# A spectral filter and a SwiGLU block in float32: two plain stripes at the start, and another share-out of the splits

## The chip, the cores and the metric

The kernel runs on one core of one Trainium2 chip. The metric is the device time of one execution in microseconds. Five engines work on their own queues: TensorE (PE, with its weight loads shown as PEld), VectorE (DVE), ScalarE (ACT), GpSimd (POOL) and SyncE (SP), which here only issues DMAs.

## The reference, cut to what matters

```python
# x: (8, 3008, 256) float32; filt_r, filt_i: (1505, 256)
X = np.fft.rfft(x, axis=1)
y = np.fft.irfft(X * (filt_r + 1j * filt_i)[None], n=3008, axis=1).astype(np.float32)
t = y.reshape(24064, 256)
g = t @ w_gate                      # w_gate, w_val: (256, 1536), w_out: (1536, 256)
silu = g * (1.0 / (1.0 + np.exp(-g)))
out = (silu * (t @ w_val) @ w_out).astype(np.float32)
```

Each batch of 3008 tokens is filtered along the sequence, then every token goes through a gated feed-forward block. The three weight matrices arrive as 64-bit floats.

## The kernel before

**The block.** The 24064 tokens are cut into 47 stripes of T = 512 tokens, the 1536 hidden columns into ND = 12 slices of 128. One stripe with one slice is a unit; there are 564. A unit does three things: `gate` (the first product, t with the slice of w_gate), `value` (t with the slice of w_val, then the Silu and the product h of both) and `project` (h times the slice of w_out, summed in PSUM over the 12 units of a stripe). The main loop goes over n and works on unit n, on the split of unit n-1 and on the projection of unit n-2.

**Triples.** The fast matmul form takes float32r, which holds fewer bits than float32. So each operand is kept as three tiles: a high part hi, a low part lo, and a combination both. Of a product of two triples, the matmuls with hi and lo go into one PSUM bank and those with the combination into another, and ScalarE (a scaling by 1/LAM) and VectorE (`axpy`, line 235) put the two together. A unit therefore has 18 matmuls of 128x128 by 128x512: ws (line 888) and wx (892) in `gate` and `value`, six each, and six in `project` (928, 930, 932). For the activations the split is: ACT scales h to hh (hi), POOL subtracts to get hl (lo, line 229), DVE's axpy makes hs (both). `split` issues the first two a unit later, `split_rest` the third two units later. The token stripes are split the same way by `split_y` into yh, yl, ys.

**PSUM.** Four banks (pool wps) serve the unit's products and the transforms, four (pool ops) the projections. Which of the four a product gets is left to the allocator; it is no fixed turn.

**Weights.** Preparation turns 64-bit weights into float32 and splits them into triples: 36 halves (12 slices by three matrices), each of 128x256, in a chain of small steps (lines 275 to 302 on DVE, 280 to 295 on ACT, 306 on POOL, then three split steps). Steps are spread over ticks: 44 ticks in the head, then three per unit. The first N_EARLY = 9 halves are loaded into the still empty y_t, the later ones into rt just before their use. Eight slices have a slot on chip (gv_t, wo_t); six of the twelve are written to DRAM (gv_all, wo_all) and streamed back for every stripe into two slots, by SP, a few units ahead.

**The early part.** Because the weights come slowly, the first FIRST = 5 stripes (batch 0 nearly whole) are visited in NG = 3 phases of DG = 4 slices: units 0 to 59. Between the phases the partial sums of a stripe go to DRAM (o_dram), come back (`load_before`) and are added on POOL (`join`).

**The transform.** Batch 0 is transformed first, alone, as matrix products (`stage1_first`, `turn`, `stage2a`, `stage2b`, `stage3`); stage3 has four quarters k, each writing every fourth group of eight tokens of y_t, so all four are needed before the first stripe. The idle matmuls (line 384) keep PE running meanwhile. Batches 1 to 7 are transformed while units run. Their steps are hung onto units by hand as hooks at places a, b, c and p of the loop body: `fold` (sums and differences on POOL), `quads`, `there` (product with the filter, with a DMA that swaps halves, and four POOL instructions), `home`, `back` (which ends in DVE transposes into y_t). A batch takes 72 units; batch b's pieces start at unit 60 + 72 (b - 2).

**Order.** `pin` keeps the program order on each engine. Each engine runs its queue in order, so a waiting instruction holds everything behind it on its engine. SP's queue holds the loads and stores of the transform, the streamed weights and the output stores; an output store is four DMAs per stripe.

Of the kernel before, what the change touches and what calls it, by code (L numbers as in the profile page):

```python
# [29 lines left out]
NH = 4  # L30
# [12 lines left out]

LAM = 4096.0
# [5 lines left out]
FIRST = 5  # L50
NG, DG = 3, 4
EARLY_UNITS = FIRST * ND
NU = NSTRIPE * ND
ORDER = (10, 4, 11, 5, 0, 6, 1, 7, 2, 8, 3, 9)
STREAM = (10, 11, 0, 1, 2, 3)
HOME = {4: 4, 5: 5, 6: 6, 7: 7, 8: 0, 9: 1}

LATER = N1 - 32
TAIL = 960


def dft_tables():
# [61 lines left out]
    return (wf.astype(f32), wi.reshape(NK, NR).astype(f32), back.astype(f32), quad.astype(f32), four.astype(f32), np.ascontiguousarray(de).astype(f32))  # L124
# [3 lines left out]
def kernel(  # L128
# [24 lines left out]
    cpool = pool("consts", 1)  # L153
    t1pool = pool("t1", 2)
    wdpool = pool("wdram", 1, DRAM)
    wps = pool("wps", 4, PSUM)
    ops = pool("ops", 4, PSUM)
# [6 lines left out]
    gv_t = [cpool.tile([128, 2, 2, 3, 128], F32R, name=f"gv_{i}") for i in range(4)]  # L164
    wo_t = [cpool.tile([128, 2, 3, 128], F32R, name=f"wo_{i}") for i in range(4)]
    y_t = cpool.tile([128, 2, S], FP32)
    y_f = y_t.rearrange("p z n -> p (z n)")
    rt = cpool.tile([128, 3072], FP32)
# [15 lines left out]
    o_dram = [wdpool.tile([128, 2, T], FP32, name=f"o_{k}") for k in range(FIRST)]  # L184
# [66 lines left out]
    raws = {}  # L251
    N_EARLY = 9
# [5 lines left out]
    def load_weights(i, queue=nc.sync):  # L258
        if i in raws or i >= len(weights):
            return  # L260
        r = y_f[:, 512 * i:512 * i + 512] if i < N_EARLY else rt[:, 512 * (i % 3):512 * (i % 3) + 512]
        raws[i] = r.bitcast(U32).rearrange("p (b f two) -> p b f two", b=2, two=2)
        pin(queue.dma_start(out=raws[i], in_=weights[i][0]))

    def round_half(i):
# [3 lines left out]
        w = rt[:, 1536 + 256 * (i % 3):1792 + 256 * (i % 3)].rearrange("p (b f) -> p b f", b=2)  # L269
        pf = rt[:, 2304 + 256 * (i % 3):2560 + 256 * (i % 3)].rearrange("p (b f) -> p b f", b=2)  # L270
# [9 lines left out]
        pin(nc.scalar.activation(out=w, in_=man, func=AF.Copy, scale=LAM * 2.0 ** -20, bias=LAM))  # L280
# [9 lines left out]
        else:  # L290
# [12 lines left out]
                                   scalar=LAM * 2.0 ** -52, in1=w.rearrange(flat),  # L303
                                   op0=ALU.mult, op1=ALU.add))
        yield
        pin(nc.gpsimd.tensor_tensor(out=w, in0=w, in1=pf, op=ALU.mult))
        yield
        t = gv_t[slot_of(d)][:, z] if z < 2 else wo_t[slot_of(d)]
        hi, lo, both = [t[:, :, n] for n in range(3)]
        pin(scaled(hi, w, DOWN / LAM))  # L310
        yield
        pin(axpy(lo, hi.bitcast(FP32), -LAM, w))
        yield
        pin(sub(nc.gpsimd, both, hi.bitcast(FP32), lo.bitcast(FP32)))

    def visit_unit(d):
        return d // DG * FIRST * DG + d % DG

    class Preparation:

        TIMES = (0, 1, 2, 3, 4, 5, 6, 7, 8, 10, 11)

        def __init__(self):
            self.at, self.ticks, self.need = 0, {}, {}
            self.barriers = []
# [3 lines left out]

            for i, (_, d, z) in enumerate(weights):  # L330
                b = 4 * i
                if i >= N_EARLY:
                    put(b - 4, lambda i=i: load_weights(i))
                half = []

                def go(half=half, i=i):
                    if not half:
                        half.append(round_half(i))
                    next(half[0], None)

                for t in self.TIMES:
                    put(b + t, go)
                by = visit_unit(d) + 2 * (z == 2)
                self.need[by] = max(self.need.get(by, 0), b + self.TIMES[-1])
                if d == 8 and z == 0:
                    self.barriers.append((b + 8, FIRST * DG + 2))
            self.end = max(self.ticks)

        def open(self, unit):
            return self.at <= self.end and all(unit >= u or self.at < t for t, u in self.barriers)  # L350

        def tick(self, unit, n=1):
            for _ in range(n):
                if not self.open(unit):
                    return
                for f in self.ticks.get(self.at, ()):
                    f()
                self.at += 1

        def finish(self, unit):  # L360
            while any(u <= unit and self.at <= t for u, t in self.need.items()):
                assert self.open(unit)
                self.tick(unit)
# [5 lines left out]
    turn_bank = [0]  # L369

    def bank(name):

        return wps.tile([128, 512], FP32, name=f"w{name}", tag="w", bufs=4)

    def head_bank(name):
        turn_bank[0] += 1
        p, tag = ((wps, "w"), (ops, "o"))[turn_bank[0] % 2]
        return p.tile([128, 512], FP32, name=f"w{name}", tag=tag, bufs=4)

    def idle(t, n, size=512):  # L380

        for i in range(n):
            ps = head_bank(f"idle")
# [3 lines left out]
    class Spectral:  # L387
# [131 lines left out]
        def stage3(self, k, step):  # L519

            i, cb = divmod(step, 2)
            ps = head_bank(f"pd_{k}_{step}")
# [5 lines left out]
            a = NW * k + NH * i  # L528
            to = y_t[:, cb].rearrange("p (r n) -> p n r", n=32)[:, a:a + NH]
            copy = (nc.scalar.copy, nc.vector.tensor_copy)[cb]  # L530
            pin(copy(out=to, in_=psv))
# [27 lines left out]
        def fold(self, g):  # L559

            if g < N_QUAD // 2:
                up, down = self.x.pop(g)
                self.x[g] = [room_of("e"), room_of("t")]
                for t, f in zip(self.x[g], (add, sub)):
                    for half in range(2):
                        a = ts(half, NV * C)
                        pin(f(nc.gpsimd, t[:, a], up[:, a], down[:, a]))
# [192 lines left out]
    with tc.tile_pool(name="start", bufs=1) as spool0:  # L760
# [12 lines left out]
        def early(tag, u):  # L773
# [10 lines left out]
                ("x", 3), ("w", 5), ("w", 6), ("w", 7), ("w", 8)] + [("t", n) for n in range(6)]  # L784
        for what, i in load:
            {"x": spec.load_x0, "w": load_weights, "t": spec.load_tables}[what](i)
        for u in range(8):
            idle(zero, 2 * (u in (4, 6)))
            spec.stage1_first(u)
            preparation.tick(0, (4, 2, 4, 2, 5, 3, 2, 6)[u])  # L790
# [4 lines left out]
        preparation.tick(0, 5)  # L795
        spec.real_part(0)
        lag = 4
        for u in range(N_TWO + lag):
            if u < N_TWO:
# [6 lines left out]
                preparation.tick(0, 2 * (u < 3))  # L806
# [11 lines left out]
            if u == 10:  # L818
                spec.load_rows(f0[0:8 * N_LOADED, 0:NW], 0, slice(0, 2 * N_LOADED), nc.gpsimd)
            if u == N_STORED + lag:  # L820
                spec.t4 = {0: f0[:, 0:NW], 1: x0_t[0], 2: x0_t[1],
                           3: lent[:, 0:NW * C].rearrange("p (n c) -> p n c", c=C)}
                for k in range(1, NCHUNK):
                    spec.load_rows(spec.t4[k][0:8 * N_STORED], k, slice(0, 2 * N_STORED))
        pin(nc.gpsimd.tensor_copy(out=one[0:NK], in_=f0[0:NK, 0, 0:1]))
        spec.store_rest(nc.gpsimd)
        for k in range(1, NCHUNK):
            spec.load_rows(spec.t4[k][8 * N_STORED:NK], k, slice(2 * N_STORED, NS),
                           (nc.sync, nc.scalar)[k % 2])
        preparation.tick(0, 5)  # L830
# [3 lines left out]
        for k in range(NCHUNK):  # L834
            for step in (0, 2, 1, 3):
                spec.stage3(k, step)
# [3 lines left out]
    wpool = pool("weights", 1)  # L840
    for i in range(4, 8):
        gv_t.append(wpool.tile([128, 2, 2, 3, 128], F32R, name=f"gv_{i}"))
        wo_t.append(wpool.tile([128, 2, 3, 128], F32R, name=f"wo_{i}"))
    ypool = pool("yp", 2)
    hpool = pool("hp", 3)
    gpool = pool("gp", 2)
    opool = pool("op", 2)

    ys = {}

    def split_y(key, a, src, first, last, fast=False):

        if key not in ys:
            ys[key] = [ypool.tile([128, 2, T], F32R, name=f"y{n}_{key}", tag=f"y{n}", bufs=2)
                       for n in ("h", "l", "s")]
        hi, lo, both = [t[:, a, first:last] for t in ys[key]]
        pin(scaled(hi, src, DOWN))
        pin(sub(nc.vector if fast else nc.gpsimd, lo, src, hi.bitcast(FP32)))
        return lambda: pin(axpy(both, lo.bitcast(FP32), -LAM, hi.bitcast(FP32)))

    class Unit:

        def __init__(self, n):
            self.n = n
            if n < EARLY_UNITS:
                visit, i = divmod(n, DG)
                self.phase, self.j = divmod(visit, FIRST)
                self.key = f"v{visit}"
                self.d = DG * self.phase + i
                self.slot = slot_of(self.d)  # L870
                self.count = DG
            else:
                stripe, i = divmod(n - EARLY_UNITS, ND)
                self.j = FIRST + stripe
                self.key = f"s{self.j}"
                self.phase = -1
                self.d = ORDER[i]
                self.item = ND // 2 * stripe + STREAM.index(self.d) if self.d in STREAM else None
                self.slot = HOME[self.d] if self.item is None else 2 + self.item % 2
                self.count = ND  # L880
            self.first, self.last = i == 0, i == self.count - 1

        def hidden(self, z):

            w, (yh, yl, yb) = gv_t[self.slot][:, z], ys[self.key]
# [10 lines left out]
        def gate(self):  # L896
            s, p = self.hidden(0)
            self.g = gpool.tile([128, T], FP32, name=f"g_{self.n}", tag="g", bufs=2)
# [3 lines left out]
        def value(self):  # L902
            s, p = self.hidden(1)
            v = gpool.tile([128, T], FP32, name=f"v_{self.n}", tag="v", bufs=1)
            pin(scaled(v, s, 1.0 / LAM))
            pin(nc.scalar.activation(out=self.g, in_=self.g, func=AF.Silu))  # L906
            pin(axpy(p, p, BOTH, v, ALU.subtract))
            self.h = gpool.tile([128, T], FP32, name=f"h_{self.n}", tag="h", bufs=2)
            pin(nc.vector.tensor_tensor(out=self.h, in0=p, in1=self.g, op=ALU.mult))  # L909

        def split(self):
            self.hs = [hpool.tile([128, T], F32R, name=f"h{k}_{self.n}", tag=f"h{k}", bufs=3)
                       for k in ("h", "l", "s")]
            pin(scaled(self.hs[0], self.h, DOWN))
            pin(sub(nc.gpsimd, self.hs[1], self.h, self.hs[0].bitcast(FP32)))
# [245 lines left out]
```

## Time and profile before

| what | value |
|---|---|
| median of 3 runs | 3023.95 us (3018.8 to 3025.24) |
| profiled execution | 3016.42 us, span of the instructions 3014.4 us, mean granted clock 0.969 |
| PE, DVE, ACT, POOL busy | 94%, 79%, 54%, 51% of the span |
| chain that ended last, by engine | PE 53%, DVE 9%, DMA 8%, issue 7%, POOL 6% |
| DMA | 587.42 MB, 195 GB/s on the mean |

How to read it: PE busy counts a matmul from its start to its modelled end, and neighbouring matmuls overlap, so 94% is no measure of how full PE is; the distance of matmul starts in the timeline is. The granted clock is given in shares of full speed. A group line shows busy time, mean length of one instruction, and the idle time of the engine before them with what ended it.

### The profile page before, as it was taken

What the parts mean: (1) busy time and instruction counts of PE and PEld (TensorE: products, weight loads), DVE (VectorE), ACT (ScalarE), POOL (GpSimd) and SP (SyncE); (2) the same over time, 40 slices, a digit from 0 to 9 for tenths busy, and PEclk for the clock granted to TensorE, in tenths of its full rate; (3) what the DMA queues carried; (4) which work ended last, traced back from release to release, by engine and by line L of the source; (5) the groups of instructions that cost most, each with busy time, mean ns of one, the idle gap of its engine ahead of it and who ended that gap; (6) DMA issues with size and microseconds to landing.
All of it is one profiled execution on the core that took longest, in us unless ns stands there. A gap on an engine that the chain in (4) does not pass through costs nothing.

```text
span 3014.4 us, 44431 instructions
## 1 busy us (share of the span) xinstructions
PE 2828.9 (94%) x14620; PEld 2062.6 (68%) x14620; DVE 2380.7 (79%) x3210; ACT 1614.8 (54%) x2907; POOL 1526.0 (51%) x1153
## 2 busy tenths in 40 slices
PE   7777889999999999999999999999999999999998
PEld 5555556677766776667766777667766677677776
DVE  6499888887887887887778788787877788787776
ACT  4355655455545555555555555455554555555554
POOL 3366665655436544474535655365553655433332
PEclk8688899999999999999999999999999999999999
DMA  8465455577756878577775777757776676744443
GB/s 184 134 227 149 133 164 137 160 228 236 230 172 201 243 225 231 159 215 235 239 207 169 225 240 227 200 176 237 221 237 180 193 231 228 223 138 150 143 152 113
DMA packets 414629, 587.42 MB, mean 195 GB/s; under 512 B 221234, under 2 KB 282064, under 8 KB 413936
## 3 DMA queue, kind: packets, MB, share of 16 engines
q1 hardware_dynamic: 413488, 582.35, 64.4%
q8 instruction: 117, 1.92, 0.3%
q0 software_dynamic: 688, 1.64, 0.2%
q14 instruction: 112, 0.92, 0.1%
q10 hardware_dynamic: 224, 0.59, 0.1%
HBM read 470.57 MB, written 109.84 MB: 193 GB/s over the span
## 4 chain that ended last, share of the span: by engine, by line
PE 53%; DVE 9%; DMA 8%; issue 7%; POOL 6%; SPq 2%; ACT 2%; DVEq 0%; POOLq 0%; ACTq 0%
PE wx L892 20%; PE ws L888 11%; PE o_s L928 6%; PE o_s L930 5%; PE o_s L932 5%; DVE hs L235 3%; DMA gv<-gv_all 2%; PE wqa L586 2%; POOL hl L229 2%; DMA lent<-d 2%; POOL yl_s L229 1%; DVE lent L693 1%; POOL lent L226 1%; SPq L404 1%; PE wpd L740 1%
## 5 line engine op out<-in xcount | busy, mean ns | idle before, releaser
L229 POOL TENSOR_TENSOR hl<-h,hh 128x512 fp32r<-128x512 f32 x564 | 765.6, 1357 | 1302.0 <-ACT hh L232 1240.6
L892 PE MATMUL wx<-yh_s,gv 128*128 128x512 f32 x2016 | 801.9, 398 | 2.9
L892 PE MATMUL wx<-yl_s,gv 128*128 128x512 f32 x2016 | 797.2, 395 | 0.0
L888 PE MATMUL ws<-ys_s,gv 128*128 128x512 f32 x2016 | 640.4, 398 | 21.1 <-DMA gv<-gv_all 8.7
L235 DVE SCALAR_TENSOR_TENSOR hs<-hl,hh 128x512 fp32r<-128x512 f32 x564 | 601.2, 1066 | 15.0 <-POOL hl L229 14.1
L232 ACT ACTIVATE hh<-h 128x512 fp32r<-128x512 f32 x564 | 356.4, 632 | 422.7 <-DVE h L909 410.9
L235 DVE SCALAR_TENSOR_TENSOR wx<-wx,v 128x512 f32<-128x512 f32 x564 | 391.2, 694 | 191.4 <-PE wx L892 169.2
L235 DVE SCALAR_TENSOR_TENSOR g<-wx,g 128x512 f32<-128x512 f32 x564 | 386.1, 685 | 187.8 <-ACT g L232 119.9
L906 ACT ACTIVATE g<-g 128x512 f32<-128x512 f32 x564 | 354.4, 628 | 326.0 <-DVE g L235 323.0
L232 ACT ACTIVATE v<-ws 128x512 f32<-128x512 f32 x564 | 337.8, 599 | 287.7 <-PE ws L888 286.7
L888 PEld LDWEIGHTS ws<-ys_s,gv 128*128 128x128 f32 x2016 | 379.4, 189 | 121.0 <-issue 14.9
L892 PEld LDWEIGHTS wx<-yh_s,gv 128*128 128x128 f32 x2016 | 381.0, 189 | 107.9 <-DVE h L909 14.9
L928 PE MATMUL o_s<-hs,wo 128*128 128x512 f32 x1008 | 427.1, 424 | 18.3 <-DVE hs L235 9.3
L892 PEld LDWEIGHTS wx<-yl_s,gv 128*128 128x128 f32 x2016 | 381.0, 189 | 89.2
L909 DVE TENSOR_TENSOR h<-wx,g 128x512 f32<-128x512 f32 x564 | 390.3, 692 | 60.2 <-DVE wx L235 1.4
L930 PE MATMUL o_s<-hh,wo 128*128 128x512 f32 x1008 | 399.1, 396 | 0.0
L932 PE MATMUL o_s<-hl,wo 128*128 128x512 f32 x1008 | 396.8, 394 | 0.0
L232 ACT ACTIVATE g<-ws 128x512 f32<-128x512 f32 x564 | 330.4, 586 | 72.9 <-PE ws L888 70.3
L928 PEld LDWEIGHTS o_s<-hs,wo 128*128 128x128 f32 x1008 | 189.2, 188 | 190.6 <-issue 89.4
L932 PEld LDWEIGHTS o_s<-hl,wo 128*128 128x128 f32 x1008 | 189.7, 188 | 44.9
L930 PEld LDWEIGHTS o_s<-hh,wo 128*128 128x128 f32 x1008 | 190.2, 189 | 30.6
L226 POOL TENSOR_TENSOR lent<-lent 128x512 f32<-128x512 f32 x140 | 191.9, 1383 | 29.8 <-DMA lent<-in_x_dram 29.8
(121 smaller groups left out, 2872.2 us busy)
## 6 DMA issues: line engine op xcount, KB each, us to landing
gv<-gv_all SPq DMA_DIRECT2D x250, 768.0 KB
wo<-wo_all SPq DMA_DIRECT2D x250, 384.0 KB
lent<-filter SPq DMA_DIRECT2D x42, 1024.0 KB
quads<-lent SPq DMA_DIRECT2D x112, 256.0 KB
lent<-quads SPq DMA_DIRECT2D x168, 128.0 KB
lent<-raw SPq DMA_DIRECT2D x168, 128.0 KB
d<-lent SPq DMA_DIRECT2D x84, 256.0 KB
lent<-d SPq DMA_DIRECT2D x112, 192.0 KB
```

Of the source, the lines that this page charges most:

```text
L226: return eng.tensor_tensor(out=dst, in0=a, in1=b, op=ALU.add)
L229: return eng.tensor_tensor(out=dst, in0=a, in1=b, op=ALU.subtract)
L232: return nc.scalar.activation(out=dst, in_=a, func=AF.Copy, scale=scale)
L235: return nc.vector.scalar_tensor_tensor(out=dst, in0=a, scalar=scale, in1=b, op0=ALU.mult, op1=op)
L586: pin(nc.tensor.matmul(out=banks[u][c:c + 32], lhsT=quad_t[r:r + NS, ts(t, 32)], rhs=parts[t][r:r + NS, ts(cp, NV * C)], start=True, stop= ...
L888: pin(nc.tensor.matmul(out=s, lhsT=w[:, a, 2], rhs=yb[:, a], start=a == 0, stop=a == 1, skip_group_check=True))
L892: pin(nc.tensor.matmul(out=p, lhsT=w[:, a, n], rhs=t[:, a], start=a + n == 0, stop=a + n == 2, skip_group_check=True))
L906: pin(nc.scalar.activation(out=self.g, in_=self.g, func=AF.Silu))
L909: pin(nc.vector.tensor_tensor(out=self.h, in0=p, in1=self.g, op=ALU.mult))
L928: pin(nc.tensor.matmul(out=s, lhsT=w[:, c, 2], rhs=both, start=self.first, stop=self.last, skip_group_check=True))
L930: pin(nc.tensor.matmul(out=p, lhsT=w[:, c, 0], rhs=hi, start=self.first, stop=False, skip_group_check=True))
L932: pin(nc.tensor.matmul(out=p, lhsT=w[:, c, 1], rhs=lo, start=False, stop=self.last, skip_group_check=True))
```

## The change

- The first PLAIN = 2 stripes (24 units) run in plain float32: their units read y_t and plain weights (plain_w, kept for six slices) directly, with 6 matmuls instead of 18, no split, one ACT instruction (Silu from PSUM) and one DVE instruction (the product from PSUM). The two stripes alternate, stripe 1 three slices behind stripe 0. The phases, the partial sums in DRAM and the joins are gone.
- Preparation makes the plain weights first, six ticks per unit, and splits them afterwards (`split_half`: ACT, POOL, DVE). Loads of later halves are issued 14 ticks ahead, N_EARLY is 8.
- Every other stripe is in triples. The split is now two ACT scalings (hi, and a second one into the tile of both) and two POOL subtractions (lo, then both from hi and lo). DVE has no part in it. In the loop, hi is scaled before unit n's gate, the rest after it.
- `fold` of the later batches moves from POOL to DVE.
- The four PSUM banks for products are taken in fixed turn.
- stage3 of batch 0 writes its quarter k as 752 tokens in a row; stage3(0) alone runs before unit 0, the other quarters at units 1 and 2, 5 and 6, 9 and 10. The output store puts batch 0's tokens back in order and has 32 to 64 DMAs for each of its stripes (32, 64, 64, 32, 64, 40).
- batch 1's row turns are issued by SP during the head; batch 1's own pieces start a unit later than before.

The core of the diff:

```diff
-FIRST = 5
-NG, DG = 3, 4
-EARLY_UNITS = FIRST * ND
+PLAIN = 2
+N_PLAIN = PLAIN * ND
+LAG = 3
...
-        r = y_f[:, 512 * i:512 * i + 512] if i < N_EARLY else rt[:, 512 * (i % 3):512 * (i % 3) + 512]
+        if i < N_EARLY:
+            r = y_t[:, i % 2, 752 + 512 * (i // 2):1264 + 512 * (i // 2)]
+        else:
+            r = rt[:, 512 * (i % 5):512 * (i % 5) + 512]
...
-                    put(b - 4, lambda i=i: load_weights(i))
+                    put(max(b - 14, 0), lambda i=i: load_weights(i))
...
-        return wps.tile([128, 512], FP32, name=f"w{name}", tag="w", bufs=4)
+        turn_bank[0] += 1
+        return wps.tile([128, 512], FP32, name=f"w{name}", tag=f"w{turn_bank[0] % 4}", bufs=1)
...
-            a = NW * k + NH * i
-            to = y_t[:, cb].rearrange("p (r n) -> p n r", n=32)[:, a:a + NH]
+            to = y_t[:, cb, NW * NR * k:NW * NR * (k + 1)].rearrange("p (r n) -> p n r", n=NW)
...
-                        pin(f(nc.gpsimd, t[:, a], up[:, a], down[:, a]))
+                        pin(f(nc.vector, t[:, a], up[:, a], down[:, a]))
...
-        pin(scaled(hi, src, DOWN))
-        pin(sub(nc.vector if fast else nc.gpsimd, lo, src, hi.bitcast(FP32)))
-        return lambda: pin(axpy(both, lo.bitcast(FP32), -LAM, hi.bitcast(FP32)))
+        split(src, [t[:, a, first:last] for t in ys[key]])
+    def split(src, parts):
+        hi, lo, both = parts
+        pin(scaled(hi, src, DOWN / LAM))
+        pin(scaled(both, src, DOWN))
+        split_rest(src, parts)
+    def split_rest(src, parts):
+        hi, lo, both = parts
+        pin(sub(nc.gpsimd, lo, src, both.bitcast(FP32)))
+        pin(sub(nc.gpsimd, both, hi.bitcast(FP32), lo.bitcast(FP32)))
...
+        def product(self, z):
+            p = bank(f"x{z}_{self.n}")
+            for a in range(2):
+                pin(nc.tensor.matmul(out=p, lhsT=plain_w[self.d][:, z, a],
+                                     rhs=y_t[:, a, ts(self.j, T)], start=a == 0, stop=a == 1,
+                                     skip_group_check=True))
+            return p
...
+            if self.plain:
+                p = self.product(0)
+                pin(nc.scalar.activation(out=self.g, in_=p, func=AF.Silu, scale=1.0 / LAM))
+                return
...
+            if self.plain:
+                p = self.product(1)
+                pin(axpy(self.h, p, 1.0 / LAM, self.g, ALU.mult))
+                return
...
-            pin(scaled(self.hs[0], self.h, DOWN))
-            pin(sub(nc.gpsimd, self.hs[1], self.h, self.hs[0].bitcast(FP32)))
-        def split_rest(self):
-            pin(axpy(self.hs[2], self.hs[1].bitcast(FP32), -LAM, self.hs[0].bitcast(FP32)))
+            pin(scaled(self.hs[0], self.h, DOWN / LAM))
+        def split_low(self):
+            pin(scaled(self.hs[2], self.h, DOWN))
+            split_rest(self.h, self.hs)
...
+        for q in range(4):
+            for a in range(4 if first else 0):
+                for k in range(NCHUNK):
+                    inside = [i for i in range(first) if 0 <= 64 * j + 4 * i + a - NR * k < NR]
+                    if inside:
+                        i0, i1 = inside[0], inside[-1] + 1
+                        r = 64 * j + 4 * i0 + a - NR * k
+                        rows(q, 8 * a, 8, i0, i1, 32 * r + NW * k, 128)
+            if first < 16:
+                rows(q, 0, 32, first, 16, T * j + 32 * first, 32)
...
+    order = [(0, i) for i in range(LAG)]
+    for i in range(ND):
+        order += [(1, i)] + [(0, i + LAG)] * (i + LAG < ND)
+    order += [(j, i) for j in range(PLAIN, NSTRIPE) for i in range(ND)]
...
-        if one_back:
-            one_back.split()
-        if two_back:
-            two_back.split_rest()
-        run_hooks(n, "b")
+        if split_now:
+            one_back.split_high()
         if u:
-            u.gate()
+            if split_now:
+                u.gate()
+                one_back.split_low()
+            run_hooks(n, "b")
+            ticks(n)
+            if not split_now:
+                u.gate()
             u.value()
```

## The prediction

> **What bounds the kernel now.** I read the page first, then the stretches (windows), the timelines of PE, DVE and SP, the groups with shapes apart, and the waits.
>
> ```profile
> PE 2828.9 (94%) x14620; PEld 2062.6 (68%) x14620; DVE 2380.7 (79%) x3210; ACT 1614.8 (54%) x2907; POOL 1526.0 (51%) x1153
> ```
> ```profile
> 100.00:150.00 50.00, 37.31 (x150) 33.35 (x149) 22.38 (x33) 18.73 (x35) 14.22 (x14) 0.57 0.39 122
> 2400.00:2500.00 100.00, 98.33 (x484) 72.83 (x474) 81.80 (x109) 57.53 (x101) 56.83 (x41) 1.00 0.75 237
> 2800.00:2900.00 100.00, 99.34 (x425) 79.19 (x424) 73.26 (x107) 57.31 (x103) 36.74 (x27) 1.00 0.47 153
> ```
> The columns are PE, PEld, DVE, ACT and POOL busy, then PE's granted clock. There are three regimes. Late (2800) PE is full: 425 matmuls, 18 to a unit, in 100 us. In the timeline its matmuls start 0.2333 us apart, so a unit takes 18 x 0.2333 = 4.20 us; measured are 4.25. In the middle (2400) PE is still the bound. Early (100) it is neither busy nor at full clock.
>
> Counting four ws matmuls per unit in the timeline, unit 0 starts at 132.2 us, unit 24 at 307.1, unit 60 at 541.8, unit 492 at 2694.7. So: head 132.2; 60 early units at 6.83; 432 units (six batches of 72) in 2152.9, that is 4.98 each; 319.7 for the last 72 and the end. In a middle batch of 359 us, units take 72 x 4.20 = 302.4, transform bursts 36.7, and distances beyond 0.2333 add up to 22.2 (mean of five batches): 9.7 around the first projection matmul (hs is late), 4.0 inside a value or gate group (a PSUM bank is late), 5 at ws (weights or ys late), the rest small. That 22 is all that a better split can win in a batch; the early part holds more.
>
> **The change, part by part.**
>
> *Head.*
> ```profile
> 96.10 7.11 PE L525 MATMUL wpd<-wi_t,f 96*128 96x94 f32 x32 [7.82 <-DMA f<-room]
> 108.58 13.94 PE L525 MATMUL wpd<-wi_t,x 96*128 96x94 f32 x64 [5.36 <-DMA x<-d]
> 132.47 1.19 PE L888 MATMUL ws<-ys_v,gv 128*128 128x512 f32 x2 [3.13 <-ACT yh_v L232]
> ```
> Unit 0 now waits for four quarters of stage3 and a split. After, it needs the first quarter alone (752 tokens of its own, plain y_t): 96.1 + 7.1 + a 0.8 us copy = 104. Against that:
> ```profile
> 57.07 0.30 DVE L275 TENSOR_SCALAR rt<-rt 128x256 uint32<-128x256 uint32 x1 [16.00 <-DMA rt<-in_moe_w_gate_dram]
> ```
> DVE stands 16 us behind the first weight half that is loaded late, whose DMA is issued after all tables (49.9 in SP's timeline). With N_EARLY 8 that half is the ninth, and its first instruction stands before stage2a(0); five stage2a instructions of 0.69 that ran before the wait (35.3 to 40.4) fall behind it: +4.5 with hops. Unit 0 at 109, a gain of 23.
>
> *24 plain units.* A plain float32 matmul of 512 columns is two records in the trace; the last twelve idle records take 5.31 us, less the overlap 0.433 each, so 0.866 per matmul. 24 units x 6 x 0.866 = 124.7. Three quarters of stage3 move between them, 3 x 3.6 (half of 7.11, which ran at half clock) = 10.8; ten transform bursts of 1.02 = 10.2. PE: 146. DVE in the same stretch: about 26 halves of four conversions (rows 0.55, 0.81, 0.76, 0.93 while POOL works; 0.45, 0.29, 0.42, 0.42 in the head), 36 split instructions (0.57 and 0.96; at best 0.4), 24 products from PSUM at 0.69, 16 folds, 17 copies and sums: 96 to 149. ACT about 90, POOL 36 x (0.89 + 0.9) + 8 x 1.45 = 76. Projections run two units behind, so PE rides over lags; I take PE with 0.5 us of gaps per unit: 158. Unit 24 at 267, 40 earlier than now. Bounds: 150, and 190 if DVE at its slow rows sets the pace.
>
> *Ten joins, ten stores and ten loads of partial sums* go; POOL joins (20 x 1.48) stood in the early part, whose gain is in the unit times above and below.
>
> *Splits.* Per triple unit DVE loses hs (1.07), ACT gains a scaling (0.63), POOL gains a subtraction.
> ```profile
> 2801.80 0.68 DVE L235 SCALAR_TENSOR_TENSOR hs<-hl,hh 128x512 fp32r<-128x512 f32 x1
> 2806.85 1.29 POOL L229 TENSOR_TENSOR hl<-h,hh 128x512 fp32r<-128x512 f32 x1 [2.87 <-ACT hh L232]
> 2807.16 1.53 DVE L235 SCALAR_TENSOR_TENSOR hs<-hl,hh 128x512 fp32r<-128x512 f32 x1
> ```
> Alone hs takes 0.68; begun while hl runs it ends 0.55 after hl does. The PSUM-fed instructions keep 0.69 beside POOL. So POOL's subtractions cost 1.29 without a fellow; means of 1.36 (hl) to 1.67 (yl) hold such waits. I take 1.29, since the opponent hs is gone and 16 folds a batch remain.
>
> The Trainium skill, "SBUF — State Buffer", section "SBUF: two separate sides", says that an instruction of VectorE with two SBUF inputs and a GpSimd instruction exclude each other for their whole length; the three rows show one side of it. By that rule each fold, which now is VectorE's, waits up to one subtraction and delays one.
>
> The Trainium skill, "GPSIMD Engine Reference", section "4.1 Engine selection", speaks against the change: it gives elementwise work with two inputs to VectorE and calls GpSimd about twice as slow. The rows agree (1.29 to 0.68); were engine time the bound, the second subtraction would cost 0.6 us per unit, 0.6 x 540 = 330 us in all.
>
> Is it the bound? Per unit POOL has 2.66 of 4.20; ACT's ring (hh, g, hs, v, silu, then DVE's h) is 3.77 of 4.20, so both fit. From the timeline: ws starts at T, hh(n-1) ends T+1.1, g's scaling T+1.56, the new scaling T+2.14, POOL hl and hs end T+4.87; the projection needs hs at T+4.20+2.77. Slack 2.1. Bursts eat it: y splits (two POOL ops each at units 3 and 5 of a stripe) beside there() (four ops over two units) give, over four units, 16 ops: lateness = 2.45 + 16 d - 20.6 (four units of 4.20, one burst of 1.02, 2.77). With d = 1.29: 2.5, three times a batch: +7.5. The folds on DVE in the quads units (sub, add, two folds, three own: 6 us and up of 4.2) eat the bank slack of 1.7: about +1 each, four: +4. Gone: hs waits but for those around bursts, -7; bank waits, as the turn is now fixed, -4; at the batch end DVE no longer holds ys back, -3. Net -2.5, I take -3 per batch, -18 in six; with d and the folds unknown, -9 to +8 per batch. Evacuation no longer stands before hs: the last 72 units -3; the drain ends in POOL (1.29) instead of DVE (0.68): +1.
>
> *Stores of batch 0.* Four DMAs per stripe become 32, 64, 64, 32, 64, 40, all on SP.
> ```profile
> 2709.90 5.67 SPq L967 DMA_DIRECT2D out_dram<-o_s  x4
> ```
> A store of now costs SP 0.67 at the median of its row, and more when DMAs back up (here 1.4). The new ones have 128 pieces; SP's rows of 32 to 128 pieces are 0.31 to 0.60. I take 0.40 (0.35 to 0.67 as bounds): bursts of 13 and 26 us. Queued behind them on SP are the raw, quads and x loads of the transform and the streamed gv and wo. Behind the raw loads waits POOL's product, and behind that the splits, hence PE. At unit 24: raw lands 19 us later, needed after 15: 2 after slack. At 27: +9. At 39: raw lands after 31.5, needed after 14.7: +15. At 51: 0. At 63 (x and gv): +7. At 75 (quads, then four): +6. Sum 39, 26 of it before unit 60; 15 to 100 at the bounds.
>
> *Units 24 to 60:* 36 x 4.20 = 151, 18 bursts 18, gaps 36 x 0.31 (as in a batch now) = 12, SP 26: 207, so unit 60 at 474 (now 541.8).
>
> **Sum.** 474 + 2152.9 - 18 + 13 + 319.7 - 2 = 2940, span before 3014.4: -74. The profiled execution took 3016.4, 7.6 under the median of its runs, 3023.95; the same offset gives 2950 us.
>
> **Rivals.**
> *Smooth* (chance 0.15): store issues hide (0.35 each, 15 in place of 39) and POOL rides over its bursts (-9 per batch in place of -3): 2950 - 24 - 36 = 2890. For it: late units sit at 4.25 with POOL at 37%.
> *SP and DVE clog the early part* (0.17), which is also the case where the plain stripes do not do what they should: 0.67 per store DMA costs 100 in place of 39, and plain units run at DVE's 190 in place of 158: 2950 + 61 + 32 = 3043 with both, 2985 with half of it. For it: prep rows are slow whenever POOL works; against: the prefetch now leads by three units.
> *POOL becomes the bound* (0.14), the slower case. Place: units 27 to 31 of each there/split meeting. Price by the same line with d = 1.6 (between yl's 1.67 and hl's 1.36): 2.45 + 25.6 - 20.6 = 7.5, three times, and about 4 at two quads meetings: +23 per batch, 6.4 batches: 2950 + 148 = 3098. It decides from about d = 1.46, where +12 per batch eats the gain. For it: yl's mean; against: hl's median is 1.30.
> *Forecast* (0.54): 2950, its own range 2900 to 3005.
>
> **Numbers.** 0.2% (6 us) is about what a measurement of this kernel can tell from no change. Faster: forecast, smooth, and 0.11 of the clog: 0.80. Same: 0.03. Slower: POOL and the rest of the clog: 0.17. Range: from the smooth case, 2880, to the clog's worst, 3040, leaving out most of POOL's case.
>
> **What the profile after would show.** Right: the first unit's matmul near 109, unit 24 near 267, plain PE records 0.43 apart, no rt wait less than 16 us; POOL near 2100 us busy and DVE near 1700; hl and hs subtractions at 1.3; batches of 72 units at 356; SP rows of out_dram at 0.4 with PE idle near units 28 to 32 and 41. Wrong: subtractions at 1.5 or more and PE waiting for POOL everywhere; unit 24 later than 300; batches over 368.

## The result, and the profile after

| kernel | median of its runs, us | ratio to the kernel before, run beside it |
|---|---|---|
| before | 3020.22 (3018.44 to 3025.24) | |
| changed | 3008.97 (3002.68 to 3012.12) | 0.9955, 95% interval 0.9939 to 0.9972 |

The changed kernel is faster by 0.45%: 14 us by the ratio, 11 by the medians. The forecast was 2950, 74 us less than the median known then: the sign was right, the size was not. The profiled execution took 3012.12 us, its span is 3010.3. It is the slowest of its five runs, so the two profiles lie only 4 us apart; the ledger below is of these two executions.

The page of the changed kernel, busy time by engine and the granted clock in 40 slices:

```profile
PE 2785.3 (93%) x14476; PEld 2047.7 (68%) x14476; DVE 1776.2 (59%) x2558; ACT 1826.4 (61%) x3433; POOL 2016.9 (67%) x1619
PEclk8998989889999999999999999999999999999999
```

The stretches of the changed kernel that answer to those of before (PE, PEld, DVE, ACT and POOL busy, granted clock, DMA share, GB/s):

```profile
100.00:150.00 50.00, 50.00 (x198) 27.30 (x198) 33.00 (x74) 29.25 (x68) 19.91 (x24) 0.92 0.86 246
2400.00:2500.00 100.00, 94.59 (x469) 70.35 (x468) 57.47 (x84) 65.50 (x123) 76.30 (x60) 0.98 0.72 225
2800.00:2900.00 100.00, 100.00 (x443) 82.80 (x442) 55.61 (x82) 72.02 (x136) 72.87 (x58) 1.00 0.48 154
```

Early (100) PE is now busy throughout, in the middle (2400) it has holes (94.59 busy in place of 98.33, clock 0.98 in place of 1.00), and late (2800) it starts 443 matmuls where it started 425. So there are a gain early, a loss in the middle, and a gain late that no step of the prediction held.

Counting matmuls per unit in the two timelines gives this ledger, in us. A batch is 72 units, the middle row is the mean of five.

| stretch | before | forecast | measured |
|---|---|---|---|
| start of unit 0 | 132.5 | 109 | 104.2 |
| start of unit 24 | 307.3 | 267 | 258.1 |
| units 24 to 59 | 234.7 | 207 | 233.3 |
| units 60 to 131 | 357.4 | 367 | 390.4 |
| each batch from unit 132 to 491 | 359.1 | 356.1 | 363.7 |
| last 72 units and end | 319.4 | 317 | 310.2 |
| span | 3014.4 | 2940 | 3010.3 |

Against the forecast: -9 before unit 24, +26 and +23 in units 24 to 131, +7.6 in each of five batches, -7 at the end, some 70 in all. Unit by unit, the loss of a batch sits in three units: unit 30 takes 11.45 us (before 6.57), unit 42 takes 12.46 (6.87), unit 54 takes 11.93 (7.49), together 14.9 more. The other 69 units win 10.3.

**The three units.** The timeline of PE and then of POOL, changed kernel, around unit 30 of a batch (start, length, line, operation, idle time ahead of it and who ended it):

```profile
1029.55 0.39 PE L977 MATMUL o<-hl,wo 128*128 128x512 f32 x1
1030.23 0.65 PE L678 MATMUL wqc<-lent 64*64 64x256 f32 x4 [0.29 <-POOL lent L237]
1034.01 1.97 PE L678 MATMUL wqc<-lent 64*64 64x256 f32 x12 [3.13 <-POOL lent L237]
1035.91 0.79 PE L974 MATMUL o<-hs,wo 128*128 128x512 f32 x1
1036.51 0.63 PE L975 MATMUL o<-hh,wo 128*128 128x512 f32 x1
1036.93 0.63 PE L977 MATMUL o<-hl,wo 128*128 128x512 f32 x1
```
```profile
1028.89 1.29 POOL L237 TENSOR_TENSOR lent<-lent 128x512 f32<-128x512 f32 x1
1030.13 1.28 POOL L240 TENSOR_TENSOR yl<-y_t,ys 128x512 fp32r<-128x512 f32 x1
1031.48 1.26 POOL L240 TENSOR_TENSOR ys<-yh,yl 128x512 fp32r<-128x512 f32 x1
1032.70 1.26 POOL L237 TENSOR_TENSOR lent<-lent 128x512 f32<-128x512 f32 x1
```

The wait is not for hs. PE stands at `home`'s matmuls (wqc), which need `there`'s last sum (line 237), and ahead of that sum POOL's queue has the two subtractions of a y split. Two things follow from this one wait: 3.13 us of idle PE, and a slow restart. Behind it matmuls of 512 columns start 0.43 us apart, not 0.2267, for about 5 us: the granted clock is 0.50 from 1034.01 to 1039.47.

The Trainium skill, "TensorE: Matmul & The Clock Gate", section "Part 1: The HAM clock gate", says that PE falls to half clock after at least one window of about 3.4 us without work and comes back after about as long at work. The trace agrees in kind, not in the numbers: here an idle time of 3.13 us was enough, and the half clock lasted 5.46 us behind it.

The group of `home`'s matmuls in the kernel before, then in the changed one (behind the bar: busy time, mean ns, idle time ahead and its releaser):

```profile
L653 PE MATMUL wqc<-lent 64*64 64x256 f32 x672 | 60.2, 403 | 12.8 <-POOL lent L226 11.6 <-POOL hl L229 1.2
```
```profile
L678 PE MATMUL wqc<-lent 64*64 64x256 f32 x672 | 90.0, 484 | 68.9 <-POOL lent L237 68.9
```

The wait was there before, small, and grew to 68.9 us over the whole kernel.

**The early stretch.** SP's queue and PE in the changed kernel, behind the end of stripe 2:

```profile
358.08 25.90 SPq L1005 DMA_DIRECT2D out_dram<-o  x64
384.08 1.31 SPq L430 DMA_DIRECT2D d<-lent  x2
385.49 3.17 SPq L430 DMA_DIRECT2D lent<-raw  x4
```
```profile
377.06 0.39 PE L924 MATMUL wx<-yl,gv 128*128 128x512 f32 x1
396.96 0.79 PE L974 MATMUL o<-hs,wo 128*128 128x512 f32 x1 [19.52 <-POOL hs L240]
```

The burst has the forecast size (64 DMAs in 25.9 us, 0.40 each). While it lasts (358 to 384 us) the DMA engines are busy for 0.31 of the time, so it is the issuing on SP that takes so long, not the moving of the data. What waits behind it was priced too low.

### The profile page after: what moved, and what is told of

Read it like the earlier page. It is cut to its first block, busy times and chain, and to the rows that moved or that the text cites. A ratio compares the mean times of both kernels' runs of the same rounds, so it can differ in the third digit from the quotient of the medians.

```text
span 3010.3 us, 44814 instructions
## 1 busy us (share of the span) xinstructions
PE 2785.3 (93%) x14476; PEld 2047.7 (68%) x14476; DVE 1776.2 (59%) x2558; ACT 1826.4 (61%) x3433; POOL 2016.9 (67%) x1619
## 4 chain that ended last, share of the span: by engine, by line
PE 56%; POOL 15%; DMA 12%; DVE 6%; SPq 4%; issue 3%; ACT 2%; POOLq 0%; DVEq 0%; ACTq 0%
PE wx L924 21%; PE ws L920 11%; PE o L974 6%; PE o L975 5%; PE o L977 5%; POOL lent L237 3%; POOL hl L240 3%; POOL hs L240 3%; DMA gv<-gv_all 3%; POOL lent L738 3%; SPq L1005 2%; PE wqc L678 2%; DMA lent<-raw 2%; PE wqa L611 2%; DMA lent<-quads 2%
## 5 line engine op out<-in xcount | busy, mean ns | idle before, releaser
L240 POOL TENSOR_TENSOR hl<-h,hs 128x512 fp32r<-128x512 f32 x540 | 710.4, 1316 | 759.0 <-ACT hs L243 726.9
L924 PE MATMUL wx<-yh,gv 128*128 128x512 f32 x2160 | 853.5, 395 | 3.3 <-DVE y_t L771 2.3
L924 PE MATMUL wx<-yl,gv 128*128 128x512 f32 x2160 | 849.8, 393 | 0.0
L240 POOL TENSOR_TENSOR hs<-hh,hl 128x512 fp32r<-128x512 f32 x540 | 705.2, 1306 | 42.3
L920 PE MATMUL ws<-ys,gv 128*128 128x512 f32 x2160 | 682.9, 398 | 49.7 <-DMA gv<-gv_all 16.0
L920 PEld LDWEIGHTS ws<-ys,gv 128*128 128x128 f32 x2160 | 412.9, 192 | 149.3 <-issue 18.1
L974 PE MATMUL o<-hs,wo 128*128 128x512 f32 x1080 | 454.7, 421 | 41.0 <-POOL hs L240 40.7
L924 PEld LDWEIGHTS wx<-yl,gv 128*128 128x128 f32 x2160 | 411.3, 190 | 85.8
L975 PE MATMUL o<-hh,wo 128*128 128x512 f32 x1080 | 429.8, 398 | 3.9 <-DVE o L246 3.9
L977 PE MATMUL o<-hl,wo 128*128 128x512 f32 x1080 | 427.5, 396 | 0.0
```

The source lines that it names most:

```text
L240: return eng.tensor_tensor(out=dst, in0=a, in1=b, op=ALU.subtract)
L920: pin(nc.tensor.matmul(out=s, lhsT=w[:, a, 2], rhs=yb[:, a], start=a == 0, stop=a == 1, skip_group_check=True))
L924: pin(nc.tensor.matmul(out=p, lhsT=w[:, a, n], rhs=t[:, a], start=a + n == 0, stop=a + n == 2, skip_group_check=True))
L974: pin(nc.tensor.matmul(out=s, lhsT=w[:, c, 2], rhs=both, stop=self.last, **kw))
L975: pin(nc.tensor.matmul(out=p, lhsT=w[:, c, 0], rhs=hi, stop=False, **kw))
L977: pin(nc.tensor.matmul(out=p, lhsT=w[:, c, 1], rhs=lo, stop=self.last, **kw))
```

## The experiments

Medians of different sets of runs come from different chips, so what is compared is each kernel's ratio to the kernel before, run beside it (its 95% interval in brackets). The changed kernel is at 0.9955; 0.001 is 3 us. Where a gain is given as two numbers, one is the difference of the ratios times 3020 us, the other the difference of the medians.

### 1. The store bursts

```diff
-        first = max(first, 0) if T * j < S else 0
+        first = 0
```

> The changed kernel, but batch 0's stripes leave in four DMAs each as all others do, so that batch 0's tokens leave in the wrong order (left out: the reordering). Theory A (the store bursts hold SP's queue, and each PE stall behind them is followed by some microseconds of matmuls at half pace): the units 24 to 81 lose their excess over the same units of later batches, which adds up to about 92 us (28 to 30: 29, 43: 23, 55: 7.5, 67: 19, 79 and 80: 10, unit 24: 3): about 2920 us against 3009. Theory B (the prediction's term): 39 us less, 2970. Theory C (the early loss comes from POOL, not from SP): no change.

2931.57 us, ratio 0.9725 (0.970 to 0.975): 69 to 77 us less than the changed kernel. Units 24 to 59 take 188.2 (233.4), units 60 to 131 take 365.3 (390.4), a middle batch 362.8 (363.7); the numbers in brackets are the changed kernel's. The result is nearest to theory A, short of its 92: what units 28 to 30 and 43 take above the same units of later batches does not all go with the bursts. These long waits of the changed kernel are gone (engine, line, what it waited for, us in total, times, longest; from three windows):

```profile
DVE lent L718 <- DMA lent<-filter: 14.6, 1, 14.6
...
PE ws L920 <- DVE lent L718: 13.0, 1, 13.0
```
```profile
PE o L974 <- POOL hs L240: 19.5, 1, 19.5
POOL lent L738 <- DMA lent<-raw: 18.0, 1, 18.0
```
```profile
ACT lent L623 <- DMA quads<-lent: 16.2, 1, 16.2
...
PE ws L920 <- ACT lent L623: 14.1, 1, 14.1
```

So three different transfers were held: the filter (behind unit 27's burst), the raw halves (unit 39's), and a store of the transform whose buffer ScalarE wants to write again (unit 63's).

### 2. The place of the y split

```diff
-                at(n - 9 + 2 * a, "b", split_y, j, a, y_t[:, a, s0:s0 + T])
+                at(n - 9 + 4 * a, "b", split_y, j, a, y_t[:, a, s0:s0 + T])
```

> The changed kernel, but the second half of each token stripe is split two units later (five units ahead of use in place of seven), away from the unit in which the transform's sums stand in POOL's queue. Theory A (in units 29, 41 and 53 of a batch POOL's queue puts two y subtractions ahead of the transform's last sum; the home matmuls of units 30, 42, 54 wait, and PE then runs at half pace for 5 us): those units fall from 11.5 to 12.5 us to about 6.2, 16 us per batch, about 95 us in all: 2914. Theory B (the prediction's price for this meeting, 7.5 per batch): 2964. Theory C (the wait is for the raw transfer and SP): no change, 3009.

2935.88 us, ratio 0.9722 (0.9682 to 0.9762): 70 to 73 us less, between theories A and B, and C falls. A middle batch takes 353.1 (363.7); units 30, 42, 54 take 7.75, 8.46 and 8.60, and the idle time ahead of wqc falls from 68.9 to 24.9 us. A change of one number, which does no less work, is worth five times the whole change.

### 3. Filling the wait

```diff
+            if self.b > 1 and w in (1, 3, 5):
+                for i in range(14):
+                    pin(nc.tensor.matmul(
+                        out=home[i % 2], lhsT=gv_t[0][:, 0, 0, 0], start=True, stop=True,
+                        rhs=gv_t[1].rearrange("p z a k n -> p (z a k n)")[:, 0:512]))
```

> The changed kernel, with 14 matmuls of 512 columns, whose results are overwritten, ahead of the home matmuls of units 30, 42 and 54 of batches 2 to 7: PE works for 3.2 us where it stood idle 3.1 us. Theory A (the idle time itself is what lowers the granted clock, and the matmuls behind it pay): the home matmuls and some six matmuls behind them run at full pace, those units lose about 2 us each, 6 per batch, 36 in all: 2972. Theory B (the half pace has nothing to do with the idle time): no change or up to 10 slower, 3009 to 3020.

2984.59 us, ratio 0.9886 (0.9861 to 0.991): 21 to 24 us less, with more work for PE. This is theory A, at about two thirds of its size. PE's timeline in this kernel at the same unit:

```profile
1016.95 3.34 PE L677 MATMUL wqc<-gv,gv 128*128 128x512 f32 x14
1020.22 0.65 PE L683 MATMUL wqc<-lent 64*64 64x256 f32 x4
1021.23 1.08 PE L683 MATMUL wqc<-lent 64*64 64x256 f32 x12 [0.36 <-POOL lent L237]
1022.24 0.50 PE L979 MATMUL o<-hs,wo 128*128 128x512 f32 x1
1022.58 0.39 PE L980 MATMUL o<-hh,wo 128*128 128x512 f32 x1
```

The twelve home matmuls take 1.08 us in place of 1.97, and the projection's first two matmuls start 0.34 us apart, not 0.60. The granted clock is 1.00 from 1021.23 to 1026.50, where it was 0.50 behind the idle time. So the idle time itself lowers the clock. Over 18 such units that is 1.2 to 1.3 us each.

### 4. The third step on DVE, and the allocator's banks

```diff
-            split_rest(self.h, self.hs)
+            pin(sub(nc.gpsimd, self.hs[1], self.h, self.hs[2].bitcast(FP32)))
+        def split_last(self):       # called behind value() of the unit
+            pin(sub(nc.vector, self.hs[2], self.hs[0].bitcast(FP32), self.hs[1].bitcast(FP32)))
```

> The changed kernel, but the last step of the split of h (both from hi and lo) is a subtraction on DVE behind the unit's product, as before the change; y and the weights keep their splits on GpSimd. Theory A (the pace of 0.2267 comes from the third split step leaving DVE): the late units go back to 4.2 or more, while units 30, 42 and 54 fall to about 7: 65 us lost, 80 won, 2995. Theory B (the pace comes from the banks' fixed turn): the late units stay at 4.08 and POOL's relief shows in full: 2925. If DVE's queue holds h back: above 3009.

2974.82 us, ratio 0.9865 (0.983 to 0.990): 27 to 34 us less. Late units take 4.10, so theory A falls. Theory B has the pace right but not the time: units 30, 42, 54 fall only to 8.7 to 9.5, and units 4, 16 and 60 take 1 us more each. At 4 and 16 PE waits for a sum of the transform on DVE, behind the new step; hence 2975 and not 2925.

```diff
-        return wps.tile([128, 512], FP32, name=f"w{name}", tag=f"w{turn_bank[0] % 4}", bufs=1)
+        return wps.tile([128, 512], FP32, name=f"w{name}", tag="w", bufs=4)
```

> The changed kernel, but the product banks are left to the allocator again. Theory A (the fixed turn is what made neighbouring matmuls start 0.2267 us apart in place of 0.2333): the late units go from 4.08 back to 4.25 us, +65 over 540 units and bank waits on top, 3075 to 3100. Theory B (the pace comes from the third split step leaving DVE): the late units stay at 4.08, only bank waits come back, up to 4 us per batch: 3009 to 3035.

(The same edit gives the head's banks back to the allocator.) 2991.48 us, ratio 0.9921 (0.9896 to 0.9947): 10 to 18 us less, which neither theory had, though this interval and the changed kernel's overlap. Late units take 4.08. The fixed turn is not the source of the pace, and no gain from it is seen.

### 5. The pace of PE

In the kernel before, late matmuls start 0.2323 us apart on the mean, in the changed one 0.2268. The diff has three padding tiles (`space`) that the prediction passed over. In the addresses that the allocator gives, the changed kernel's split weights, y and h triples all lie at 64 modulo 512 bytes; before, the triples lay at 128, four weight slots at 128 and four at 32.

```diff
         space(pool, 416)
+        space(pool_on(left, "off_a", 1, "left"), 32)
+        pool = pool_on(left, "weights_off", 1, "left")
         for i in range(8):
...
+        space(pool_on(left, "off_b", 1, "left"), 32)
```

> The changed kernel, but the on-chip slots of the split weights begin 32 bytes later, so that their addresses are 32 past a multiple of 64; all other tiles stay where they were. Theory A (the pace of matmul starts hangs on where the weights lie: in the kernel before, half of the slots lay 32 bytes off and PE started every 0.2333 us; in the changed one all lie on 64 and it is 0.2267): late units go from 4.08 to 4.20 or 4.25 us, +65 us over 540 units: 3070. Theory B (the pace has another cause): late units stay at 4.08, 3009.

3021.11 us, ratio 1.0009 (0.9996 to 1.0023). Matmuls start 0.2333 apart and late units take 4.20: theory A for the pace. The padding also moved the y triples, to 128, which the expectation did not say; the weights (at 96) are 32 bytes off the y and the h triples alike. The whole loses 12 to 16 us, not 61. The last 72 units lose 8, but a middle batch takes 364.0 against 363.7: most ordinary units are 0.1 longer, and units 30, 42, 54 are 0.8 to 1.6 shorter. The reading that fits is that a slower PE only comes later to the same wait for POOL.

```diff
+    cpool.tile([128, 8], FP32, name="space")
     gv_t = [cpool.tile([128, 2, 2, 3, 128], F32R, name=f"gv_{i}") for i in range(4)]
...
     one = cpool.tile([128, 1], FP32)
+    cpool.tile([128, 8], FP32, name="space2")
```

> The kernel before, but with 32 bytes of padding ahead of the first four weight slots and 32 behind the constants, so that every weight slot begins on a multiple of 64 bytes. Theory A (the weights' place sets the pace): late units fall from 4.25 to about 4.1, about 0.12 us for most of 564 units: 60 us less, 2955. Theory B (another cause): no change, about 3015.

3011.54 us, ratio 0.9977 (0.9963 to 0.9992); late units 4.25, starts 0.2315 apart. That is nearly theory B. But in gate and value the units on the four slots that agree with the triples (192 modulo 512) have 0.227 to 0.229, those on the other four (64 against 192) 0.232 to 0.233.

Next, the small tiles g, v, h: 32 bytes of padding ahead of them on top of the last kernel, and, the other way round, away from them in the changed kernel.

> The kernel before with the weight slots on multiples of 64 bytes (as tried already, which left the late units at 4.25 us) and, new, the small tiles g, v, h of ScalarE and VectorE 32 bytes past a multiple of 64, as they lie in the changed kernel. Theory A (PE starts every 0.2267 us only where its operands and the small tiles of the other engines lie 32 bytes apart in their place modulo 64): late units 4.08 to 4.1, 50 to 70 us less than 3012: 2945 to 2960. Theory B (the place of g, v, h has no part in it): late units stay at 4.2 or more, 3012.

> The changed kernel, but g, v, h lie on multiples of 64 bytes like all operands of PE; nothing else moves. Theory A (the other engines' tiles must lie 32 bytes apart from PE's operands): late units go from 4.08 to 4.2 or more and the whole to about 3020, as with the weights moved. Theory B (only PE's own operands count): late units 4.08, about 3009.

Before: 3009.60, ratio 0.9971 (0.9954 to 0.9988), starts 0.2315. Changed: 3002.18, ratio 0.9942 (0.9924 to 0.9959), starts 0.2268. Theory B holds in both; these tiles have no part in it. What was left is the place of PE's two operands to each other:

```diff
+    cpool.tile([128, 24], FP32, name="space")      # ahead of gv_t, in the kernel before
+    cpool.tile([128, 104], FP32, name="space2")    # behind `one`
```

> The kernel before with 96 bytes of padding ahead of the weight slots and 416 behind the constants, so that all weight slots, ys, yl, yh, hs, hl, hh lie at the same place modulo 512 (128), as they all lie at 64 in the changed kernel. Theory A (PE starts every 0.2267 us where weights and moving tiles agree modulo 512; it explains why four of eight slots were nearly fast in the kernel before and in the padded one): late units 4.08 in place of 4.25, last 72 units 310 in place of 319, 55 to 80 us less in all: 2940 to 2965. Theory B (padding has no part in it): 4.2 or more, 3010.

And, in the changed kernel, 128 and 384 bytes in place of the 32 and 32 around the weights:

> The changed kernel with its weight slots moved by 128 bytes: on a multiple of 64, but at 192 modulo 512 where the moving tiles lie at 64. Theory A (agreement modulo 512): late units 4.20, about 3020 as with the weights moved by 32. Theory B (a multiple of 64 is enough): late units 4.08, 3005.

The kernel before with agreeing places: starts 0.2270 apart, 2999.85 us, ratio 0.9908 (0.9878 to 0.9939). The changed kernel with weights at 192 against 64: starts 0.2324, 3033.09 us, ratio 1.0009 (0.9990 to 1.0028). Theory A holds for the pace, twice. For the time in the kernel before it promised two to three times too much (55 to 80 us, measured 28): a middle batch there won 2.3 us, the last 72 units 5.7. The stretch 2800 to 2900 of these two, as above (the first number behind an x counts PE's matmuls; before 425, changed 443):

```profile
2800.00:2900.00 100.00, 99.00 (x434) 80.72 (x433) 74.13 (x109) 58.35 (x105) 37.95 (x28) 1.00 0.45 152
```
```profile
2800.00:2900.00 100.00, 100.00 (x432) 81.04 (x432) 54.42 (x80) 71.39 (x132) 71.81 (x57) 1.00 0.47 153
```

So the two padded places are worth 0.9% to the old kernel, more than the whole change, and without its pace the changed kernel is no faster than before.

### 6. Both costs taken away

The store's DMAs are collected in a list and issued over 20 units (12 for the first stripe), with the y split of experiment 2:

```diff
-                at(end + 1, "a", store, u)
+                jobs = store(u)
+                for i, job in enumerate(jobs):
+                    at(end + 1 + ((20 if u.j else 12) * i // len(jobs) if len(jobs) > 4 else 0), "a", job)
```

> The changed kernel with both causes taken away: the second y split two units later, and the store DMAs of a stripe of batch 0 spread over 20 units (12 for the first stripe) in place of one burst; tokens in the right order. Theory A (the two costs are separate and each was its own: 77 and 73 us in the runs so far): 3009 - 77 - 73 = 2859, at most 15 above it if spread issues cost SP something. Theory B (both act through the same waits): 2900 or more.

2885.32 us, ratio 0.9561 (0.9533 to 0.9589): 119 us less than the changed kernel, against 140 by the sum of the two ratios, so between theory A (2859 to 2874) and theory B. Units 24 to 59 take 208.4 us, against 188.2 with four stores; that spread stores still take SP's time there is a reading of this. Then POOL was relieved further: y splits at 11 and 5 units ahead, and the third step of h on DVE in six units of a batch.

> The version with spread stores (2885), with the two y splits at 11 and 5 units ahead of use, and with the third step of h on DVE in the six units of a batch whose subtractions stand with the transform's four GpSimd instructions. Theory A (what is left at units 30, 42, 54, 7.6 to 8.0 us, is still POOL's queue): they fall to 5.4 to 6, 6 us per batch, 38 in all: 2847. Theory B (the rest is the home matmuls' own time and hops): 2880 to 2890.

2864.73, ratio 0.9489 (0.9445 to 0.9533): 22 us less, somewhat over half of theory A. Units 30, 42, 54: 6.37, 7.60, 6.95. With the allocator's banks:

> The same, with the product banks left to the allocator. Theory A (the fixed turn costs, as the 18 us between 3009 and 2991 suggested): 15 to 20 us less than the run beside it. Theory B (the 18 us were chips and scatter): the same within 6 us. The prediction's term (the fixed turn saves 4 us a batch): 25 us more.

2851.60, ratio 0.9454 (0.9429 to 0.948): 11 to 13 us less in the same set of runs, between the theories and nearer to A; with four runs each the two intervals overlap. Last, the stores, those of the later stripes too, at the end of a unit (place c in place of a):

> The version of 2852 with the spread store DMAs issued at the end of a unit, behind the unit's own loads, in place of its start. Theory A (the spread stores still hold loads back in units 24 to 60, 206 us there against 188 with four stores): 5 to 15 us less, 2840. Theory B (what is left there is SP's time as a whole, not the order in a unit): 2852.

2839.85, ratio 0.9374 (0.9353 to 0.9395). The spans of the profiles differ by 8.8 us, 3.6 of it in units 24 to 59, the medians by 12 and the ratios by 24 (another set, another chip): less, but by how much is open. Units 30, 42, 54 take 5.34, 5.50 and 5.32, and units 59 and 60 give back 1.2 us each. This version beats both kernels: 6.3% under the one before.

## Why the prediction was right or wrong

**Head.** Right, 5 us too careful. DVE awaits a weight half for longer than before (idle 26.3 us, was 16.0), but wpd starts at 97.35, 1.25 later than before, where +4.5 was put. The first quarter of stage3 and a copy do follow, and unit 0 starts at 104.2 (96 to 103 in the other profiles of the changed kernel's versions).

**24 plain units.** Right: 153.9 us against 158. Their PE records start 0.43 us apart, as forecast.

**The subtractions on POOL.** Right in price (1.316 and 1.306 against 1.29), wrong in place. This is the first failed step. The rival "POOL becomes the bound" named the meeting of `there` and the y split at units 27 to 31, and the sum measured POOL's lateness against the time at which the *projection* needs hs. But `home`'s matmuls, which need `there`'s last sum, stand in PE's queue ahead of the second half of that projection, and this sum is behind both y subtractions. The row that said so was in the profile before: 11.6 us of idle PE ahead of wqc, released by `there`'s sum on POOL. And each wait was priced at its own length only; the restart at half pace adds 1.2 to 1.3 us (experiment 3). So the three meetings cost 14.9 us per batch where 7.5 was put, with d, the length of a subtraction, at 1.31. By the prediction's own line 14.9 would need a d of 1.44, so the cost did not come from slow subtractions but from the order in the queue.

**Folds on DVE.** Oversized, as far as the units tell: +4 per batch was put on the quads units. Of units 2 to 15 three got longer (10, 14 and 15, by 2.4 us together), the others shorter, unit 6 by 2.6 for a reason that was not followed. The folds take 1.31 to 1.33 us on the mean where DVE's PSUM-fed sums take 0.69; that they wait for POOL fits this, but no run tests it.

**hs waits.** Right for ordinary units: in units such as 2, 27, 33, 39, 51 the first projection matmul starts 0.23 us behind the matmul ahead of it, where it was 0.51 to 0.57. These units are 0.46 to 0.49 shorter, some 0.1 of it the pace.

**Banks.** Wrong: -4 per batch was put, and no gain is seen. Leaving the turn to the allocator again makes the kernel 10 to 18 us faster in one pair of runs and 11 to 13 in another; as the intervals overlap in both, a loss from the fixed turn is likely rather than shown.

**Store bursts.** The second failed step. Size of the bursts right (0.40 each, 25.9 us), price of what is queued behind them not: 39 was put, 69 to 77 measured. By the unit of the burst, put, and measured as what went with four stores (experiment 1): 24: 2 and 0; 27: 9 and 19; 39: 15 and 19; 51: 0 and 8; 63: 7 and 19; 75: 6 and 10. At 27 and 63 the raw halves, x and gv were followed, but the filter load and the transform's own store, both on the same queue, were not. At 51 the streamed gv was counted as early enough and was 6 us late. These waits, too, have a slow restart behind them: the granted clock is 0.50 there (at 27, from 285.1 to 295.3).

**What the sum did not hold.** The pace: 0.0055 us per matmul. It alone keeps the result under the kernel before (experiment 5), and it is worth 12 to 16 us, since in the batches most of it is lost again at the waits. The prediction used 0.2333 for both kernels; the trace of before held starts of 0.227 beside those of 0.238, and the diff held the padding.

**The sum.** Some 70 us between the two spans: 49 in units 24 to 131 (stores, first of all, and batch 1's and 2's meetings), 38 in five batches (meetings 7.4 per batch above price, no bank gain, less the pace), less 9 at the start and 7 at the end. How the 7.6 of a batch divide between bank turn, pace and waits is not told apart beyond this. Two slips in the prediction's numbers carry nothing: its unit starts (132.2, 307.1, 541.8, 2694.7) are 0.2 to 0.3 early against the matmul rows, and half of the clog's 93 us gives some 2996, not 2985.

## What to carry to other kernels

When an instruction is added to a busy queue, follow each later instruction of that queue to the engine that awaits it, and take the first that PE's queue reaches, not the one whose work was changed; the groups' idle column shows small waits of today that grow. The same holds for a burst on a DMA queue: list every load and store behind it, also stores that free a buffer. And a difference of 2% in the start distance of the same matmul is a clue to follow, not a constant.

## What the runs showed of the hardware

- The distance of starts of 128x128 by 128x512 float32r matmuls depends on the place of the weights to the moving tile: 0.2267 to 0.2270 us where all agree modulo 512 bytes (64 and 64, 128 and 128), 0.232 to 0.2345 on the mean where they are 32, 96 or 128 bytes apart. Whether the period is 256, 512 or 1024 is not told apart.
- The pace comes back slowly. Behind the half clock above, the changed kernel's matmuls from 1039.49 on start 0.231, 0.234, 0.235, 0.224, 0.231, 0.236, 0.228, 0.234 and 0.230 us apart, then 0.226 to 0.227. In the kernel before, the units on the four slots at 128 have 0.2295 to 0.2302 on the mean in gate and value, with 0.227 only in the last matmuls of `value`. Why it takes so many matmuls is not shown.
- An idle time of 3.13 us in PE is followed by some 5 us of matmuls at half pace (granted clock 0.50). Fourteen useless matmuls in that gap, at 18 places, made the kernel 0.7% faster.
